# Decoding order in the first block, a smaller sum of squares, and a third decoding ahead of the first transposes

## The chip, the cores and the metric

The program runs on one core of a Trainium2 chip. The metric is the device time of one execution in microseconds (us). The engines named below are TensorE (PE, matrix products), VectorE (DVE), ScalarE (ACT), GpSimd (POOL) and SyncE (SP, whose queue starts the DMA transfers). Each of them works through its own list of instructions in the order written, and semaphores hold an instruction until what it needs is there.

## The reference

Local-plus-global attention is followed by two feed-forward layers. There are 4 batches of 512 local and 32 global tokens, 2176 in all, and 8 heads of 64, so the width is 512.

```python
s_ll = where(|i - j| <= 32, 0.125 * q_l @ k_l.T, -1e9)          # window of 32 on either side
out_l = softmax([0.125 * q_l @ k_g.T, s_ll]) @ [v_g, v_l]
out_g = softmax(0.125 * q_g @ [k_g, k_l].T) @ [v_g, v_l]
x = [out_g, out_l] as (2176, 512)
h = x @ w_in                                  # 512 -> 2048
x = where(h > 0, h, exp(min(h, 0)) - 1) @ w_out          # 2048 -> 512
xn = x / sqrt(mean(x * x) + 1e-6) * rms_g
g = xn @ w_gate;  out = (g * sigmoid(g) * (xn @ w_val)) @ w_o2      # 512 -> 1536 -> 512
```

The weights reach the chip as 64-bit floats, and the kernel decodes them there into 32-bit floats by integer operations.

## The kernel before

**Numbers as two halves.** Every operand of a large product is kept as a high half in the format fp32r and a low half (what the high half leaves over), and a product is three matmuls: high by high, high by low, low by high (`PASSES`). ScalarE makes a high half by a copy, VectorE the low half by a subtraction.

**Decoding a weight piece.** A piece holds 2 x 128 rows by 512 columns. `dec_abs` (line 79, ScalarE) takes the absolute value of the upper word into `dx`; `dec_bits` (lines 86 to 89, VectorE) clamps, shifts, and puts in the sign and the low bits; `w1_hi` (line 92, ScalarE) makes the high half in `wA`, `w1_lo` (line 95, VectorE) the low half. Each waits for the one before. In the text a decoding's six instructions are called abs, clamp, shift, sign, low bits (the four of `dec_bits`), and then high and low. Sixteen pieces (0 to 15) belong to the first layer: in each group of four (`order1`) two pieces of `w_in`, needed by four steps of the block, and two of `w_out`, each needed by two steps.

**Order of the first layer.** The attention of the first block's four units (0 to 3) is computed in a list written out by hand, with pieces 0 to 2 laid between. Then `moe_block` runs for four blocks of 512 tokens with 16 steps each. Step j computes `h` (12 matmuls, line 128), its activation on ScalarE and VectorE (`elu_a`, lines 117 to 119, then `g`, lines 135 and 136), and the second product of the step before (`y`, 12 matmuls, line 142). Beside it, every four steps take one unit of the next block's attention: scores `s` and their row maxima (lines 229 and 230) and exponentials `E` (line 232) at the first step, transposes and their copies `ET` (line 240) at the second, the product with v at the third. In block 0 every step 0 to 12 ends with `w1_decode`, which decodes one more piece (3 to 15) and starts a later transfer.

**What sets the order.** TensorE's list is in program order throughout, and in the first stretch (the list by hand) ScalarE's and VectorE's too. From block 0 on, a scheduler orders the instructions of ScalarE and VectorE by when it reckons them ready; with `tc.keep_in_program_order` an instruction may not move ahead of those written before it on its engine. Blocks 1 and 2 decode the second layer's weights (with that mark already) and store them to memory, from where the second layer fetches them (`w2_fetch`).

**Second layer.** `prep` makes the normalised `xn` in four parts: load, sum of squares over the four column groups (ScalarE squares, GpSimd adds into `acc`), a product with a matrix of ones that sums over partitions (`ms`, line 558), and the scaling.

Of the kernel before, what the change touches and what calls it, by code (L numbers as in the profile page):

```python
# [34 lines left out]
def i32(ap):  # L35
    return ap.bitcast(I32)
# [3 lines left out]
def fused_kernel(ctx: ExitStack, tc: tile.TileContext, kq, vl, gkq, gv, w_in, w_out, w_gate, w_val, w_o2, rms_g, consts, out):  # L40
# [36 lines left out]
    def dec_abs(pool, raw, keep=False):  # L77
        x = pool.tile([P, 1024], F32, tag="dx", name="dx")
        ins = nc.scalar.activation(x, f(words(raw)[:, :, 1]), AF.Abs)  # L79
        if keep:  # L80
            tc.keep_in_program_order(ins)
        return x

    def dec_bits(x, raw):
        word = words(raw)
        nc.vector.tensor_scalar(out=x, in0=x, scalar1=HI_MIN, scalar2=HI_MAX, op0=ALU.max, op1=ALU.min)
        nc.vector.tensor_scalar(out=i32(x), in0=i32(x), scalar1=3, scalar2=0x3FFFFFFF, op0=ALU.logical_shift_left, op1=ALU.bitwise_and)
        nc.vector.scalar_tensor_tensor(out=i32(x), in0=word[:, :, 1], scalar=-0x40000000, in1=i32(x), op0=ALU.bitwise_and, op1=ALU.bitwise_or)  # L88
        nc.vector.scalar_tensor_tensor(out=i32(x), in0=word[:, :, 0], scalar=29, in1=i32(x), op0=ALU.logical_shift_right, op1=ALU.bitwise_or)  # L89

    def split_hi(dst, t):
        nc.scalar.copy(dst[:, :, 0, :], t.rearrange("p (a n) -> p a n", a=2))
# [80 lines left out]
    with ExitStack() as ls:  # L173
# [176 lines left out]
        dxs, dsts = {}, {}  # L350

        def w1_abs(i):
            dxs[i] = dec_abs(dec["t"], raws[i])

        def w1_bits(i):
            dec_bits(dxs[i], raws.pop(i))

        def w1_hi(i):
            kind, a, G = order1[i]
# [9 lines left out]
        def w1_lo(i):  # L369
            split_lo(dsts.pop(i), dxs.pop(i))  # L370
            n_dec[0] = i + 1
# [14 lines left out]
        with tc.manual_schedule(engines={mybir.EngineType.DVE, mybir.EngineType.Activation}):  # L386
            nc.scalar.copy(identr, ident)
            nc.scalar.copy(masks, mk)
            load_kq(1)
            load_v(1)  # L390
            w1_load()
            load_kq(2)
            load_v(2)
            load_kq(3)
            load_v(3)
            w1_load(3)
            w1_abs(0)
            a_S(0, ATT2)
            w1_bits(0)
            a_E(0)  # L400
            a_S(1, HB)
            a_T(0, 0, yps, "y0")
            a_T(0, 1, yps, "y1")
            w1_hi(0)
            a_E(1)
            a_PV(0, Y2)
            w1_lo(0)
            a_N(0)
            w1_abs(1)
            a_S(2, ATT2)  # L410
            a_T(1, 0, yps, "y0")
            a_T(1, 1, yps, "y1")
            a_E(2)
            w1_bits(1)
            a_PV(1, Y2)
            a_N(1)
            a_S(3, HB)
            a_T(2, 0, yps, "y0")
            a_T(2, 1, yps, "y1")
            a_E(3)  # L420
            w1_hi(1)
            a_PV(2, Y2)
            a_N(2)
            a_T(3, 0, yps, "y0")
            a_T(3, 1, yps, "y1")
            w1_lo(1)
            w1_abs(2)
            a_PV(3, Y2)
            a_N(3)
            xT_t = {0: new_xT()}  # L430
            a_X(0, (0, 1), xT_t[0], ATT2[:2] + HB)
            last = a_X(0, (2, 3), xT_t[0], ATT2[:2] + HB)
            w1_bits(2)
            w1_hi(2)
            w1_lo(2)
        w1_load(2)
# [21 lines left out]
        def slot0(j, part, h):  # L458
            g = act1(h, 512, elu_a) if part == 0 else None
            att_slot(0, j, part)  # L460
            if part == 2:
                with tc.issue_after(last[0].ins), tc.issue_after(last[1].ins):
                    w1_decode()
                if j == 12:
                    w2_load()
                    w2_load()
            return g
# [24 lines left out]

    def second_start():
        bpools["bp"] = ctx.enter_context(tc.tile_pool(name="bp", bufs=1))
        bpools["ones"] = bpools["bp"].tile([P, P], F32, name="ones")
        nc.sync.dma_start(out=bpools["ones"], in_=consts[:, 4 * P:5 * P])
        bpools["gg"] = stage.enter_context(tc.tile_pool(name="ggp", bufs=2))
        bpools["st"] = stage.enter_context(tc.tile_pool(name="bst", bufs=4))
        prep(0, 0)
        w2_fetch()  # L500

    wraws, n_fetch = [], [0]

    def w2_fetch():
        while len(wraws) < 4 and n_fetch[0] < 18:
            raw = bpools["st"].tile([P, 1024], F32, tag="wraw", name="wraw")
            i = n_fetch[0]
            nc.sync.dma_start(out=raw.rearrange("p (a n) -> p a n", a=2), in_=wT[2 * i:2 * i + 2].rearrange("a p n -> p a n"))
            wraws.append(raw)
            n_fetch[0] += 1  # L510
# [24 lines left out]
    def prep(k, part):  # L535
# [8 lines left out]
        elif part == 1:  # L544
# [3 lines left out]
            for c in range(1, 4):  # L548
# [3 lines left out]
                    sq = moe.tile([P, 512], F32, tag="e", name="sq", bufs=2)  # L552
                nc.scalar.activation(sq[:, :n], y32[:, c, :n], AF.Square)
                nc.gpsimd.tensor_tensor(out=acc[:, :n], in0=acc[:, :n], in1=sq[:, :n], op=ALU.add)
            acc_t[k] = acc
        elif part == 2:
            ms = hps.tile([P, 512], F32, tag="h", name="ms")
            nc.tensor.matmul(ms[:, :n], bpools["ones"], acc_t[k][:, :n], start=True, stop=True)
            rs = stg.tile([P, 512], F32, tag="stg", name="rs")
            nc.scalar.activation(rs[:, :n], ms[:, :n], AF.Sqrt, bias=eps, scale=1.0 / DM)  # L560
            nc.vector.reciprocal(rs[:, :n], rs[:, :n])
# [349 lines left out]
```

## Time and profile before

| what | us |
|---|---|
| median of 3 runs (lowest, highest) | 949.61 (947.6, 949.84) |
| the profiled execution's own time | 949.2 |
| its span, first to last instruction | 947.3 |
| TensorE busy in the span | 915.8 |
| VectorE busy in the span | 459.7 |
| ScalarE busy in the span | 347.0 |

Durations of single instructions come from the profiled execution, so sums are made against its 949.2 us. A table by stretches gives for each engine the time in which it was busy and, behind x, the instructions begun in it; `PEclk` is the granted TensorE clock as a share of full speed. In a timeline, a number in brackets at a row's end is the time for which the engine was idle ahead of it and what ended that.

### The profile page before, as it was taken

How to read it: one execution, taken by the hardware profiler on the slowest of the kernel's cores; microseconds unless marked ns; L12 is line 12 of the kernel's file. 1: busy time of each engine (PE TensorE's matmuls, PEld its weight loads, DVE VectorE, ACT ScalarE, POOL GpSimd, SP SyncE). 2: the span in 40 equal slices, each digit the busy share in tenths (PEclk: the TensorE clock that was granted, in tenths of full speed). 3: DMA queues.
4: the chain of work that ended last, by engine and by line, in shares of the span. 5: the costliest groups of instructions: out<-in, count | busy, mean ns of one | idle time of the engine just before them, and what ended most of it. 6: DMA issues, size and time to landing. Idle time of an engine off the chain costs nothing.

```text
span 947.3 us, 15710 instructions
## 1 busy us (share of the span) xinstructions
PE 915.8 (97%) x6738; PEld 766.5 (81%) x6738; DVE 459.7 (49%) x791; ACT 347.0 (37%) x627; POOL 17.9 (2%) x19
## 2 busy tenths in 40 slices
PE   6788899999999999999999999999999999999997
PEld 5566688888887788777888888888889999999996
DVE  4799963666578874543786215221412241142111
ACT  4577544434443443332656213122312232232111
POOL 0000000000000000000100100001000100100000
PEclk9999999999999999999999999999999999999999
DMA  9675541544567763351644000100011010000000
GB/s 364 250 297 188 178 163 57 181 170 166 187 223 277 276 232 127 124 184 57 243 137 157 12 1 5 41 33 1 1 34 45 1 34 34 1 1 34 1 1 34
DMA packets 34445, 107.77 MB, mean 114 GB/s; under 512 B 3016, under 2 KB 5704, under 8 KB 31816
## 3 DMA queue, kind: packets, MB, share of 16 engines
q1 hardware_dynamic: 34376, 106.77, 31.5%
q8 instruction: 53, 0.87, 0.4%
q14 instruction: 16, 0.13, 0.0%
HBM read 88.41 MB, written 18.35 MB: 113 GB/s over the span
## 4 chain that ended last, share of the span: by engine, by line
PE 84%; DVE 8%; DMA 3%; issue 2%; ACT 2%; SPq 0%; ACTq 0%
PE y L142 15%; PE pg L633 15%; PE pv L633 15%; PE y L639 15%; PE h L128 14%; DVE dx L88 1%; DVE dx L89 1%; PE o L251 1%; PE yg L597 1%; PE s L221 1%; PE hg L581 1%; PE ptp L238 1%; DMA kq<-in_kq 1%; PE s L216 1%; DVE wA L95 1%
## 5 line engine op out<-in xcount | busy, mean ns | idle before, releaser
L142 PE MATMUL y<-g,wA 128*128 128x512 f32 x768 | 198.8, 402 | 6.1 <-DVE g L136 5.7
L128 PE MATMUL h<-xT,wA 128*128 128x512 f32 x768 | 186.8, 392 | 1.3 <-DVE xT L276 1.3
L142 PEld LDWEIGHTS y<-g,wA 128*128 128x128 f32 x768 | 140.2, 189 | 40.9 <-DVE g L136 8.4
L128 PEld LDWEIGHTS h<-xT,wA 128*128 128x128 f32 x768 | 144.2, 189 | 32.3 <-DVE xT L276 1.5
L806 DVE TENSOR_TENSOR silu<-pv,silu 128x384 f32<-128x384 f32 (+1 forms) x60 | 36.7, 611 | 257.2 <-PE pv L633 249.1
L639 PE MATMUL y<-wB,p 128*128 128x512 f32 x612 | 149.0, 391 | 0.0
L639 PEld LDWEIGHTS y<-wB,p 128*128 128x128 f32 x612 | 114.4, 188 | 22.3
L805 ACT ACTIVATE silu<-pg 128x384 f32<-128x384 f32 (+1 forms) x60 | 32.1, 534 | 158.9 <-PE pg L633 158.7
L633 PE MATMUL pv<-xT,wB 128*128 128x384 f32 (+1 forms) x432 | 88.4, 352 | 0.0
L633 PEld LDWEIGHTS pv<-xT,wB 128*128 128x128 f32 x432 | 77.3, 188 | 5.6
L808 ACT CAST p<-silu 128x384 fp32r<-128x384 f32 (+1 forms) x60 | 33.3, 555 | 127.0 <-DVE silu L806 126.8
L135 ACT CAST g<-e 128x512 fp32r<-128x512 f32 x64 | 39.8, 622 | 75.8 <-DVE e L111 71.0
L633 PE MATMUL pv<-xnB,wB 128*128 128x512 f32 (+1 forms) x288 | 61.5, 362 | 0.0
L109 ACT ACTIVATE e<-h 128x512 f32<-128x512 f32 x48 | 28.9, 601 | 85.3 <-PE h L128 77.9
L633 PE MATMUL pg<-xT,wB 128*128 128x384 f32 (+1 forms) x288 | 60.1, 357 | 0.0
L633 PEld LDWEIGHTS pg<-xT,wB 128*128 128x128 f32 x288 | 52.1, 188 | 5.8 <-issue 0.5
L633 PEld LDWEIGHTS pv<-xnB,wB 128*128 128x128 f32 x288 | 52.2, 188 | 5.6
L809 DVE TENSOR_TENSOR p<-silu,p 128x384 fp32r<-128x384 f32 (+1 forms) x60 | 38.0, 634 | 35.5 <-ACT p L808 35.5
L110 DVE TENSOR_SCALAR e<-e 128x512 f32<-128x512 f32 x52 | 22.2, 428 | 65.2 <-ACT e L109 65.0
L136 DVE TENSOR_TENSOR g<-e,g 128x512 fp32r<-128x512 f32 x64 | 45.1, 705 | 17.6 <-ACT g L135 16.3
L79 ACT ACTIVATE dx<-raw 128x1024 f32<-128x1024 f32 x34 | 39.5, 1162 | 10.9 <-DMA raw<-in_moe_w_out 4.3
L232 ACT ACTIVATE E<-s,mx 128x128 f32<-128x128 f32 x128 | 35.1, 384 | 22.3 <-DVE mx L230 22.3
(179 smaller groups left out, 948.5 us busy)
## 6 DMA issues: line engine op xcount, KB each, us to landing
raw<-in_moe_w_out SPq DMA_DIRECT2D x14, 1024.0 KB, 6.1
wT<-dx SPq DMA_DIRECT2D x18, 512.0 KB, 3.4
wraw<-wT SPq DMA_DIRECT2D x18, 512.0 KB, 4.2
raw<-in_moe_w_in SPq DMA_DIRECT2D x8, 1024.0 KB, 7.2
raw<-in_moe_w_gate SPq DMA_DIRECT2D x6, 1024.0 KB, 6.2
raw<-in_moe_w_val SPq DMA_DIRECT2D x6, 1024.0 KB, 6.8
gvr<-in_gv SPq DMA_DIRECT2D x8, 640.0 KB, 4.6
gkq<-in_gkq SPq DMA_DIRECT2D x4, 1152.0 KB, 5.2
```

What stands on the lines that cost most here:

```text
L79: ins = nc.scalar.activation(x, f(words(raw)[:, :, 1]), AF.Abs)
L128: nc.tensor.matmul(h[:, :n], W1[c, G][:, ws, o:o + P], xT[c][:, xs, :n], start=(k == 0), stop=(k == 11))
L135: nc.scalar.copy(g[:, 0, :n], e[:, :n])
L136: nc.vector.tensor_tensor(out=g[:, 1, :n], in0=e[:, :n], in1=f(g[:, 0, :n]), op=ALU.subtract)
L142: nc.tensor.matmul(ys[dc][:, :n], W2[j][:, ws, dc * P:(dc + 1) * P], g[:, gs, :n], start=(j == 0 and k == 0), stop=(j == 15 and k == 2))
L232: nc.scalar.activation(e[par][:, pr, :], ss[par][:, pr, :], AF.Exp, bias=mx[:, par, pr:pr + 1], scale=SCALE)
L633: nc.tensor.matmul(ps[:, :n], W[c, G3][:, ws, o:o + P], xn[c][:, xs, :n], start=(k == 0), stop=(k == 11))
L639: nc.tensor.matmul(os_[t], p[:, pp, t * P:(t + 1) * P], Wo[j][:, ww, :], start=(j == 0 and k == 0), stop=(j == 11 and k == 2))
L805: nc.scalar.activation(s[:, :n], pg[:, :n], AF.Silu)
L806: nc.vector.tensor_tensor(out=s[:, :n], in0=pv[:, :n], in1=s[:, :n], op=ALU.mult)
L808: nc.scalar.copy(p[:, 0, :n], s[:, :n])
L809: nc.vector.tensor_tensor(out=p[:, 1, :n], in0=s[:, :n], in1=f(p[:, 0, :n]), op=ALU.subtract)
```

## The change

Four things change. First, in block 0 the abs of pieces 3 to 15 carries the mark that keeps it in ScalarE's written order, and `w1_decode` as a whole is held back behind one instruction of the last transposes instead of two. Second, the decoding of piece 2 moves in the list by hand from behind the transposes of x to between the last attention units: its abs ahead of the exponentials of unit 3, its four bit steps apart among the normalisations of units 2 and 3. Third, the sum of squares is split into high and low halves and multiplied by fp32r ones in two matmuls, where one fp32 matmul stood. Fourth, the ones are set by GpSimd instead of being loaded, and the buffers for the fetched weights go from 4 to 3.

```diff
--- before.py
+++ after.py
@@ -81,12 +81,16 @@
             tc.keep_in_program_order(ins)
         return x
 
-    def dec_bits(x, raw):
+    def dec_bits(x, raw, steps=range(4)):
         word = words(raw)
-        nc.vector.tensor_scalar(out=x, in0=x, scalar1=HI_MIN, scalar2=HI_MAX, op0=ALU.max, op1=ALU.min)
-        nc.vector.tensor_scalar(out=i32(x), in0=i32(x), scalar1=3, scalar2=0x3FFFFFFF, op0=ALU.logical_shift_left, op1=ALU.bitwise_and)
-        nc.vector.scalar_tensor_tensor(out=i32(x), in0=word[:, :, 1], scalar=-0x40000000, in1=i32(x), op0=ALU.bitwise_and, op1=ALU.bitwise_or)
-        nc.vector.scalar_tensor_tensor(out=i32(x), in0=word[:, :, 0], scalar=29, in1=i32(x), op0=ALU.logical_shift_right, op1=ALU.bitwise_or)
+        if 0 in steps:
+            nc.vector.tensor_scalar(out=x, in0=x, scalar1=HI_MIN, scalar2=HI_MAX, op0=ALU.max, op1=ALU.min)
+        if 1 in steps:
+            nc.vector.tensor_scalar(out=i32(x), in0=i32(x), scalar1=3, scalar2=0x3FFFFFFF, op0=ALU.logical_shift_left, op1=ALU.bitwise_and)
+        if 2 in steps:
+            nc.vector.scalar_tensor_tensor(out=i32(x), in0=word[:, :, 1], scalar=-0x40000000, in1=i32(x), op0=ALU.bitwise_and, op1=ALU.bitwise_or)
+        if 3 in steps:
+            nc.vector.scalar_tensor_tensor(out=i32(x), in0=word[:, :, 0], scalar=29, in1=i32(x), op0=ALU.logical_shift_right, op1=ALU.bitwise_or)
 
     def split_hi(dst, t):
         nc.scalar.copy(dst[:, :, 0, :], t.rearrange("p (a n) -> p a n", a=2))
@@ -350,10 +354,10 @@
         dxs, dsts = {}, {}
 
         def w1_abs(i):
-            dxs[i] = dec_abs(dec["t"], raws[i])
-
-        def w1_bits(i):
-            dec_bits(dxs[i], raws.pop(i))
+            dxs[i] = dec_abs(dec["t"], raws[i], keep=i > 2)
+
+        def w1_bits(i, steps=range(4)):
+            dec_bits(dxs[i], raws[i] if 3 not in steps else raws.pop(i), steps)
 
         def w1_hi(i):
             kind, a, G = order1[i]
@@ -417,20 +421,22 @@
             a_S(3, HB)
             a_T(2, 0, yps, "y0")
             a_T(2, 1, yps, "y1")
+            w1_abs(2)
             a_E(3)
+            w1_bits(2, (0, 1))
             w1_hi(1)
             a_PV(2, Y2)
             a_N(2)
             a_T(3, 0, yps, "y0")
             a_T(3, 1, yps, "y1")
+            w1_bits(2, (2,))
             w1_lo(1)
-            w1_abs(2)
             a_PV(3, Y2)
             a_N(3)
+            w1_bits(2, (3,))
             xT_t = {0: new_xT()}
             a_X(0, (0, 1), xT_t[0], ATT2[:2] + HB)
             last = a_X(0, (2, 3), xT_t[0], ATT2[:2] + HB)
-            w1_bits(2)
             w1_hi(2)
             w1_lo(2)
         w1_load(2)
@@ -459,7 +465,7 @@
             g = act1(h, 512, elu_a) if part == 0 else None
             att_slot(0, j, part)
             if part == 2:
-                with tc.issue_after(last[0].ins), tc.issue_after(last[1].ins):
+                with tc.issue_after(last[1].ins):
                     w1_decode()
                 if j == 12:
                     w2_load()
@@ -492,17 +498,17 @@
 
     def second_start():
         bpools["bp"] = ctx.enter_context(tc.tile_pool(name="bp", bufs=1))
-        bpools["ones"] = bpools["bp"].tile([P, P], F32, name="ones")
-        nc.sync.dma_start(out=bpools["ones"], in_=consts[:, 4 * P:5 * P])
+        bpools["ones"] = bpools["bp"].tile([P, P], F32R, name="ones")
+        nc.gpsimd.memset(f(bpools["ones"]), 1.0)
         bpools["gg"] = stage.enter_context(tc.tile_pool(name="ggp", bufs=2))
-        bpools["st"] = stage.enter_context(tc.tile_pool(name="bst", bufs=4))
+        bpools["st"] = stage.enter_context(tc.tile_pool(name="bst", bufs=3))
         prep(0, 0)
         w2_fetch()
 
     wraws, n_fetch = [], [0]
 
     def w2_fetch():
-        while len(wraws) < 4 and n_fetch[0] < 18:
+        while len(wraws) < 3 and n_fetch[0] < 18:
             raw = bpools["st"].tile([P, 1024], F32, tag="wraw", name="wraw")
             i = n_fetch[0]
             nc.sync.dma_start(out=raw.rearrange("p (a n) -> p a n", a=2), in_=wT[2 * i:2 * i + 2].rearrange("a p n -> p a n"))
@@ -552,10 +558,15 @@
                     sq = moe.tile([P, 512], F32, tag="e", name="sq", bufs=2)
                 nc.scalar.activation(sq[:, :n], y32[:, c, :n], AF.Square)
                 nc.gpsimd.tensor_tensor(out=acc[:, :n], in0=acc[:, :n], in1=sq[:, :n], op=ALU.add)
-            acc_t[k] = acc
+            a2 = bpools["bp"].tile([P, 2, 512], F32R, tag="a2", name="a2")
+            nc.scalar.copy(a2[:, 0, :n], acc[:, :n])
+            nc.vector.tensor_tensor(out=a2[:, 1, :n], in0=acc[:, :n], in1=f(a2[:, 0, :n]), op=ALU.subtract)
+            acc_t[k] = a2
         elif part == 2:
             ms = hps.tile([P, 512], F32, tag="h", name="ms")
-            nc.tensor.matmul(ms[:, :n], bpools["ones"], acc_t[k][:, :n], start=True, stop=True)
+            acc = acc_t[k]
+            for i in range(2):
+                nc.tensor.matmul(ms[:, :n], bpools["ones"], acc[:, i, :n], start=(i == 0), stop=(i == 1))
             rs = stg.tile([P, 512], F32, tag="stg", name="rs")
             nc.scalar.activation(rs[:, :n], ms[:, :n], AF.Sqrt, bias=eps, scale=1.0 / DM)
             nc.vector.reciprocal(rs[:, :n], rs[:, :n])
```

The names in the next rows are the program's: `e_1061` is the activation of step 5 in block 0, `e_957` that of step 4, `E_1009` and `E_1010` the exponentials of attention unit 5, and `dx_1037`, `dx_1094`, `dx_1180` hold pieces 7, 8 and 9.

ScalarE in steps 4 and 5 of block 0, before:

```order
L79 ACTIVATE dx_1037<-raw_755 128x1024
L117 ACTIVATE e_914<-h_901 128x512
L118 ACTIVATE e_914<-e_914 128x512
L135 CAST g_918<-e_914 128x512
L92 CAST wA_939<-dx_933 128x2x512
L117 ACTIVATE e_957<-h_944 128x512
L118 ACTIVATE e_957<-e_957 128x512
L79 ACTIVATE dx_1094<-raw_812 128x1024
L92 CAST wA_1043<-dx_1037 128x2x512
L135 CAST g_961<-e_957 128x512
L79 ACTIVATE dx_1180<-raw_899 128x1024
L232 ACTIVATE E_1009<-s_964,mx_1008 128x128 x4
```

ScalarE at the same place in the changed kernel:

```order
L139 CAST g_961<-e_957 128x512
L236 ACTIVATE E_1009<-s_964,mx_1008 128x128 x4
L236 ACTIVATE E_1010<-s_965,mx_1008 128x128 x4
L79 ACTIVATE dx_1037<-raw_755 128x1024
L121 ACTIVATE e_1061<-h_1048 128x512
L96 CAST wA_1043<-dx_1037 128x2x512
L122 ACTIVATE e_1061<-e_1061 128x512
L244 COPY ET_1079<-ptp_1074 128x512
L244 COPY ET_1086<-ptp_1081 128x512
L79 ACTIVATE dx_1094<-raw_812 128x1024
L139 CAST g_1065<-e_1061 128x512
L121 ACTIVATE e_1118<-h_1105 128x512
```

The abs of piece 7 (`dx_1037`) stood ahead of step 3's activation and now stands behind the exponentials of step 4. The abs of piece 8 (`dx_1094`) stood in step 4 and now stands in step 5, behind the copies `ET` and ahead of that step's `g_1065`; the abs of piece 9 is no longer in the first six steps.

VectorE from the low half of piece 6 on, before:

```order
L95 TENSOR_TENSOR wA_939<-dx_933,wA_939 128x2x512
L89 SCALAR_TENSOR_TENSOR dx_1037<-raw_755,dx_1037 128x1024
L119 SCALAR_TENSOR_TENSOR e_957<-e_957,h_944 128x512
L86 TENSOR_SCALAR dx_1094<-dx_1094 128x1024
L95 TENSOR_TENSOR wA_1043<-dx_1037,wA_1043 128x2x512
L229 TENSOR_REDUCE mx_1008<-s_964 128x4
L87 TENSOR_SCALAR dx_1094<-dx_1094 128x1024
L229 TENSOR_REDUCE mx_1008<-s_965 128x4
L136 TENSOR_TENSOR g_961<-e_957,g_961 128x512
L230 TENSOR_SCALAR mx_1008<-mx_1008 128x4
L86 TENSOR_SCALAR dx_1180<-dx_1180 128x1024
L88 SCALAR_TENSOR_TENSOR dx_1094<-raw_812,dx_1094 128x1024
```

VectorE at the same place in the changed kernel:

```order
L99 TENSOR_TENSOR wA_939<-dx_933,wA_939 128x2x512
L140 TENSOR_TENSOR g_961<-e_957,g_961 128x512
L233 TENSOR_REDUCE mx_1008<-s_964 128x4
L233 TENSOR_REDUCE mx_1008<-s_965 128x4
L234 TENSOR_SCALAR mx_1008<-mx_1008 128x4 x2
L87 TENSOR_SCALAR dx_1037<-dx_1037 128x1024
L89 TENSOR_SCALAR dx_1037<-dx_1037 128x1024
L91 SCALAR_TENSOR_TENSOR dx_1037<-raw_755,dx_1037 128x1024
L93 SCALAR_TENSOR_TENSOR dx_1037<-raw_755,dx_1037 128x1024
L99 TENSOR_TENSOR wA_1043<-dx_1037,wA_1043 128x2x512
L123 SCALAR_TENSOR_TENSOR e_1061<-e_1061,h_1048 128x512
L87 TENSOR_SCALAR dx_1094<-dx_1094 128x1024
```

Before, steps of two or three pieces alternate and lie between the row maxima (`mx_1008`). Now the maxima come in one run, then the whole of piece 7 in a row, its bit steps and its low half next to each other, and only then the activation of step 5.

ScalarE ahead of the first block, before:

```order
L232 ACTIVATE E_497<-s_438,mx_496 128x128 x4
L232 ACTIVATE E_498<-s_439,mx_496 128x128 x4
L92 CAST wA_511<-dx_318 128x2x512
L240 COPY ET_559<-ptp_554 128x512
L240 COPY ET_566<-ptp_561 128x512
L79 ACTIVATE dx_569<-raw_129 128x1024
L275 CAST xT0_612<-xtp_616 128x512
L275 CAST xT1_613<-xtp_623 128x512
L275 CAST xT2_614<-xtp_630 128x512
L275 CAST xT3_615<-xtp_637 128x512
L79 ACTIVATE dx_746<-raw_131 128x1024
```

ScalarE at that place in the changed kernel:

```order
L79 ACTIVATE dx_496<-raw_129 128x1024
L236 ACTIVATE E_499<-s_438,mx_498 128x128 x4
L236 ACTIVATE E_500<-s_439,mx_498 128x128 x4
L96 CAST wA_515<-dx_318 128x2x512
L244 COPY ET_563<-ptp_558 128x512
L244 COPY ET_570<-ptp_565 128x512
L279 CAST xT0_616<-xtp_620 128x512
L279 CAST xT1_617<-xtp_627 128x512
L279 CAST xT2_618<-xtp_634 128x512
L279 CAST xT3_619<-xtp_641 128x512
L96 CAST wA_648<-dx_496 128x2x512
```

The abs of piece 2 (`dx_569`, now `dx_496`) has moved from behind the copies of unit 3 to ahead of its exponentials, and the abs of piece 3 no longer follows the four casts of xT.

## Rows read from the trace of the kernel before

**Rows 1.** The page: busy time by engine, and the group of all abs instructions.
```profile
PE 915.8 (97%) x6738; PEld 766.5 (81%) x6738; DVE 459.7 (49%) x791; ACT 347.0 (37%) x627; POOL 17.9 (2%) x19
...
L79 ACT ACTIVATE dx<-raw 128x1024 f32<-128x1024 f32 x34 | 39.5, 1162 | 10.9 <-DMA raw<-in_moe_w_out 4.3
```

**Rows 2.** Table by stretches: length, PE, PEld, DVE, ACT, POOL busy, PEclk, DMA.
```profile
43.20:118.40 75.20, 66.28 (x616) 51.91 (x614) 74.96 (x105) 49.22 (x80) 0.00 (x0) 0.98 0.58 209
71.84:102.95 31.11, 27.61 (x251) 21.73 (x250) 31.07 (x45) 21.64 (x33) 0.00 (x0) 1.00 0.55 193
102.95:134.02 31.07, 28.56 (x251) 22.82 (x250) 26.79 (x38) 17.82 (x31) 0.00 (x0) 0.95 0.54 194
134.02:162.33 28.31, 28.31 (x267) 23.43 (x266) 10.64 (x23) 12.51 (x27) 0.00 (x0) 1.00 0.19 65
189.06:215.58 26.52, 26.52 (x252) 21.77 (x250) 16.80 (x30) 9.91 (x21) 0.00 (x0) 1.00 0.54 192
```

**Rows 3.** TensorE's longest wait from 42 to 135 us: total, times, longest.
```profile
PE y L142 <- DVE g L136: 5.3, 4, 2.5
```

**Rows 4.** Chain of waits around two products with ones: start, duration, what.
```profile
481.29 2.72 PE y L142 x12
484.87 2.97 PE h L128 x12
...
675.27 2.72 PE y L639 x12
678.64 2.77 PE pg L633 x12
```

**Rows 5.** Timeline ahead of block 0: start, duration, engine, line, tiles.
```profile
32.72 0.59 ACT L240 COPY ET<-ptp 128x512 f32<-128x512 f32 x1 [2.41 <-PE ptp L238]
33.22 2.17 ACT L232 ACTIVATE E<-s,mx 128x128 f32<-128x128 f32 x8
...
37.11 1.29 ACT L79 ACTIVATE dx<-raw 128x1024 f32<-128x1024 f32 x1
...
42.63 3.01 PE L128 MATMUL h<-xT,wA 128*128 128x512 f32 x12 [1.29 <-DVE xT L276]
```

**Rows 6.** VectorE's groups by line, 43.2 to 118.4 us: busy, mean ns.
```profile
L88 DVE SCALAR_TENSOR_TENSOR dx<-raw,dx 128x1024 int32<-128x1024 int32 x13 | 15.9, 1226 | 0.1
L89 DVE SCALAR_TENSOR_TENSOR dx<-raw,dx 128x1024 int32<-128x1024 int32 x12 | 14.6, 1217 | 0.0
L95 DVE TENSOR_TENSOR wA<-dx,wA 128x1024 fp32r<-128x1024 f32 x12 | 14.6, 1216 | 0.0
L87 DVE TENSOR_SCALAR dx<-dx 128x1024 int32<-128x1024 int32 x13 | 8.9, 688 | 0.1
L86 DVE TENSOR_SCALAR dx<-dx 128x1024 f32<-128x1024 f32 x13 | 8.8, 685 | 0.1
```

**Rows 7.** Timeline: one high half, then one undisturbed step of block 0.
```profile
49.02 1.05 ACT L92 CAST wA<-dx 128x1024 fp32r<-128x1024 f32 x1 [2.07 <-DVE dx L89]
...
136.94 0.60 ACT L117 ACTIVATE e<-h 128x512 f32<-128x512 f32 x1 [2.81 <-PE h L128]
137.57 0.63 ACT L118 ACTIVATE e<-e 128x512 f32<-128x512 f32 x1
138.24 0.69 DVE L119 SCALAR_TENSOR_TENSOR e<-e,h 128x512 f32<-128x512 f32 x1 [3.37 <-ACT e L118]
138.96 0.62 ACT L135 CAST g<-e 128x512 fp32r<-128x512 f32 x1 [0.75 <-DVE e L119]
140.22 1.28 DVE L229 TENSOR_REDUCE mx<-s 128x4 f32<-128x512 f32 x2
141.67 2.17 ACT L232 ACTIVATE E<-s,mx 128x128 f32<-128x128 f32 x8 [2.10 <-DVE mx L230]
```

**Rows 8.** Table by stretches of 1 us, columns as in rows 2.
```profile
55.00:56.00 1.00, 1.00 (x5) 0.69 (x4) 1.00 (x2) 1.00 (x5) 0.00 (x0) 0.50 1.08 444
...
121.00:122.00 1.00, 1.00 (x4) 0.74 (x3) 0.97 (x2) 1.00 (x3) 0.00 (x0) 0.50 0.47 147
```

## The prediction

> **What bounds the kernel now.** I read the page first: TensorE is busy for 915.8 of 947.3 us [rows 1], so time is to be had where it idles, or by taking work from it. The table by stretches says where it idles. Four steps late in the first layer take 26.52 us and TensorE works through all of it: that is what four steps with one attention unit cost when nothing is late. In block 0 the same piece of work took 31.11 us in steps 4 to 7 and 31.07 in steps 8 to 11, and from step 12 to the end of the block 28.31 us without idling [rows 2]. VectorE was busy for 74.96 of the 75.20 us from 43.20 to 118.40. So block 0 is held by VectorE's queue, and the longest single wait of TensorE there is for the low half of g, up to 2.5 us [rows 3]. That queue holds the decoding of the weights: a piece costs it 0.69 + 0.69 + 1.23 + 1.22 + 1.22 = 5.0 us [rows 6].
>
> **The change part by part.**
>
> *Products with ones.* From the start of a y product to the start of the next one with an ordinary one between (12 matmuls, 2.72 us, 0.227 each) there are 3.58 us in two cases and 3.37 in three: the fp32 product costs 0.86 us at 512 columns and 0.65 at 384 [rows 4]. Two fp32r matmuls cost 2 x 0.227 = 0.45, or 0.34 at 384 by the share of columns. Gain: 2 x 0.41 + 3 x 0.31 = 1.7 us, all on TensorE's path, since it idles nowhere there. The Trainium skill, "FP8 and Floating Point Precision", TensorE Precision Notes, says that a true fp32 product makes four passes through the array; by that a product would cost 4 x 0.227 = 0.91 us and the gain would be 1.9 instead of 1.7; the rows, at 3.8 passes, decide. The halves added for it are a ScalarE copy as for g (0.62, rows 7) and a VectorE subtraction (half of the 1.22 of a low half of double size, rows 6, so 0.6), five times. They lie between two parts of `prep` that are two steps of TensorE's products apart; without that cover each would cost 1.2 us. Ones by a memset and three buffers in place of four: a fetch starts one piece later. No row prices that; the nearest is a high half's 1.05 us [rows 7], by which a late piece would push what is queued behind it. I take 0, bounds -0.3 and +1.0.
>
> *Piece 2 ahead of x.* On ScalarE its abs (1.16 us, rows 1) now stands between the copies of unit 2's transposes and the eight exponentials of unit 3, which started at once when it was not there [rows 5]. Behind them queue unit 3's transposes, its product with v, x and xT: all of it 1.1 us later. On VectorE the last bit step (1.22) lies between x and the low halves of xT and adds 0.2. So block 0 starts 1.3 us later than 42.63. Bounds: 0, if the exponentials had slack that the trace doesn't show, and +5, if the raw weights landed only just before 37.11, where their abs ran in the kernel before (37.11 - 33.22 = 3.9 more).
>
> *Steps 0 to 3.* VectorE no longer has eight bit steps of pieces 2 and 3 ahead of the first g, and the 2.5 us wait goes. Late next: the attention product of step 2, by 0.4, and the g of step 2, by 1.1 us, behind the bit steps of piece 4. From the first h to the h of step 4: 26.52 less one y product (2.72) that step 0 doesn't have, plus 1.5, is 25.3 us; the trace has 71.84 - 42.63 = 29.2. Gain 3.9.
>
> *From step 4 on: ScalarE's order.* The trace's timeline follows the printed order row by row on both engines, so I laid the rows' durations end to end along it, each instruction starting when its predecessor and what it needs are done. Two things happen. The abs now follows the exponentials, so VectorE sits idle after the row maxima for 2.2 + 1.16 us, and where a piece's low half follows its bit steps directly it waits again for the high half (1.05, rows 7): idle time put into the queue that was 99% busy. And a decoding of the second w_in piece of a group (5, 9, 13) has only one step of lead, so TensorE stands in the middle of h in steps 4, 8 and 12 until its high and low half are there. The chain from that wait in step 8 to the one in step 12, with small latencies in the terms:
> rest of h 0.9; activation 0.60 + 0.63, high and low half of piece 10 and g low, 4.3 in all; row maxima 1.4; exponentials 2.2; abs 1.1; the four bit steps 3.9; high half 1.1; activation 0.5 and two copies 1.0; abs 1.1, clamp 0.7, g low 0.6; the rest of y 2.5 and h 2.7; wait for an abs 0.4, activation 1.3, then its VectorE part behind shift and sign 1.9 + 0.7, g high 0.6; abs 1.1, high half of piece 13 1.0; behind a shift 0.4, low half 1.2 [rows 6, 7]. Sum 32.6 us, against 31.07 traced and 26.52 undisturbed. From step 4 to 8 it is 1.7 more, since the wait in step 4 is 4.8 us (high half 3.6, low half 1.2) instead of 3.1, piece 5's abs standing behind the late g of step 2 and its high half behind the g of step 3 and one more abs: 34.3 against 31.11. Behind step 12, 28.31 plus that step's wait of 3.1.
>
> *Sum.* +1.3 - 3.9 + 3.2 + 1.5 + 3.1 = +5.2 us in block 0. The same laying of the kernel before ends its block at 160.0 us where the trace has 162.33; 1.0 of that is the clock (below), the other 1.3 are latencies too small to list, and I add them. The granted clock stood at 0.50, that is at 1.2 instead of 2.4 GHz, in the microseconds after two stretches of waiting, near 55 and 121 us [rows 8]. A mean clock of 0.95 over the 31.07 us of steps 8 to 11 [rows 2] is 1.6 us lost to such a stretch. Behind the wait in step 4, longer than the longest now [rows 3], I expect it again; part of it falls where TensorE would wait anyway, and I take 1.0. Together +7.5, less 1.7: 949.2 + 5.8 = 955.0 us. The profiled execution's 949.2 is 0.4 below the median of 949.61, which I leave out.
>
> **The rivals.**
>
> *Half clock behind all three waits.* The Trainium skill, "TensorE: Matmul & The Clock Gate", Part 1, has it that the half-rate clock is the default and activity releases it, so that idling brings it back; what it would make of the time is this rival. For it: the trace has it twice already [rows 8], and the waits in steps 8 and 12 are 3.1 us with two matmuls between their parts. Two more stretches, each costing its whole 1.6 because behind them nothing else is late, make 3.2: 958.2. Against it: the waits there are shorter than that of step 4, and TensorE's mean clock from 43.20 to 118.40 was 0.98 though it idled for 8.9 us [rows 2].
>
> *VectorE's sum decides.* Its 3.8 us for piece 2 leave block 0, and if the rest stays as dense as now, TensorE's 8.9 us of idling shrink by that: 949.2 - 3.8 + 1.3 - 1.7 = 945.0. For it: 74.96 of 75.20 us. It decides if VectorE idles in the block for less than those 3.8 us. Against it: in the printed order the maxima, the exponentials, the abs and the bit steps form one chain with nothing of VectorE's between, four times over.
>
> *A trade.* The new waits only replace those for g, as they do up to step 4, where the changed kernel is ahead by 3.9 - 1.3 = 2.6 us. It decides when the waits in steps 4, 8 and 12 are 2 us each instead of 4.8, 3.1 and 3.1: of the 7.5 us there remain 2.5, and the products take 1.7 back: 950.0. For it: a tenth or two too much in each of the 23 terms would do. Against it: the h of step 4 has its wait for both halves written in the middle of its products, and their predecessors are not ready.
>
> **How the numbers follow.** Forecast 0.50 (952.5 to 957.5), half clock three times 0.19, trade 0.18, VectorE's sum 0.13. A measurement of this kernel tells 0.3%, 2.9 us, from no change: slower is above 952.5. So slower 0.69, same 0.18, faster 0.13. The range from 948.5 to 959.5 leaves out the faster rival and the ends of the others; the likeliest case alone spans 952.5 to 957.5.
>
> **What would show it.** In the profile after: h of step 4 should be cut in two by a wait for the high half (ScalarE) of 3 to 4 us and one of about 1 for the low half, and likewise shorter in steps 8 and 12; VectorE should be idle for some 3 us after each run of row maxima in block 0 and busy clearly below 99% there; block 0 should begin near 44.0 us and end near 168 to 172 instead of 162.33; the products with ones should take half as long. If VectorE stays fully busy to 118 us, or TensorE passes step 4 without a wait, the forecast is wrong; if block 0 begins after 45 us, the transfer of piece 2 was late.

## The result and the profile after

The changed kernel took 958.64 us in the median of three runs (957.34 to 960.8) against 949.61 us. The ratio is 1.0105, 95% interval 1.0077 to 1.0134, so it is slower by about 1%. Its profiled execution took 957.34 us, with a span of 955.4.

The first table by stretches has the approach to block 0 and then its four groups of steps (steps 0 to 3, 4 to 7, 8 to 11, 12 to the end), columns as in [rows 2]. The groups end at the first `h` of steps 4, 8, 12 and of block 1.

```profile
38.00:45.05 7.05, 5.83 (x80) 4.86 (x80) 6.48 (x12) 2.98 (x7) 0.00 (x0) 0.52 0.25 70
45.05:70.63 25.58, 24.69 (x238) 19.58 (x239) 18.63 (x30) 15.72 (x28) 0.00 (x0) 1.00 0.56 204
70.63:106.01 35.38, 30.44 (x252) 23.30 (x250) 28.61 (x41) 18.15 (x30) 0.00 (x0) 0.90 0.51 183
106.01:139.48 33.47, 29.16 (x251) 22.78 (x250) 27.64 (x40) 18.28 (x31) 0.00 (x0) 0.95 0.34 117
139.48:171.89 32.41, 30.46 (x267) 24.31 (x266) 22.41 (x35) 17.77 (x32) 0.00 (x0) 0.95 0.45 153
```

Block 0 begins at 45.05 us instead of 42.63 [rows 5] and ends at 171.89 instead of 162.33 [rows 2]: 9.56 us lost. Behind it the kernel takes 783.51 us against 784.97, 1.46 less. Steps 0 to 3 gained 3.63 us against this row of the kernel before:

```profile
42.63:71.84 29.21, 26.29 (x238) 20.50 (x239) 29.11 (x43) 18.86 (x31) 0.00 (x0) 0.94 0.64 242
```

Against [rows 2], the later groups lost 4.27, 2.40 and 4.10. VectorE, full before in the first two groups of steps, is now idle for 7 us in each; in the third it is idle for 6 us, where it was for 4.

The table of waits in block 0 of the changed kernel names what TensorE and VectorE waited for (total, times, longest). TensorE:

```profile
PE h L132 <- ACT wA L96: 6.0, 3, 3.3
PE h L132 <- DVE wA L99: 2.3, 3, 0.9
PE y L146 <- DVE g L140: 2.1, 4, 0.8
PE y L146 <- ACT g L139: 1.2, 2, 1.0
```

VectorE:

```profile
DVE dx L87 <- ACT dx L79: 15.0, 7, 3.2
DVE wA L99 <- ACT wA L96: 3.7, 7, 1.1
```

Waits for g fell from 5.3 us [rows 3] to 3.3, and `h` now waits 8.3 us for weights, which it did not in the kernel before; and VectorE now waits 15.0 us for an abs, where the kernel before had this:

```profile
DVE dx L86 <- ACT dx L79: 0.4, 1, 0.4
```

The timeline at the first row maxima shows how:

```profile
51.38 1.28 DVE L233 TENSOR_REDUCE mx<-s 128x4 f32<-128x512 f32 x2
52.58 0.28 DVE L234 TENSOR_SCALAR mx<-mx 128x4 f32<-128x4 f32 x2
52.83 2.18 ACT L236 ACTIVATE E<-s,mx 128x128 f32<-128x128 f32 x8 [2.09 <-DVE mx L234]
54.85 1.20 ACT L79 ACTIVATE dx<-raw 128x1024 f32<-128x1024 f32 x1
56.08 0.70 DVE L87 TENSOR_SCALAR dx<-dx 128x1024 f32<-128x1024 f32 x1 [3.21 <-ACT dx L79]
```

Maxima, eight exponentials, abs, clamp stand in one chain, and VectorE has nothing else in it. TensorE's timeline in the `h` of steps 4, 8 and 12, and, between the last two, ahead of the `y` that stands in step 10 and takes the g of step 9:

```profile
75.49 1.22 PE L132 MATMUL h<-xT,wA 128*128 128x512 f32 x2 [3.34 <-ACT wA L96]
77.15 2.08 PE L132 MATMUL h<-xT,wA 128*128 128x512 f32 x4 [0.44 <-DVE wA L99]
...
109.21 0.73 PE L132 MATMUL h<-xT,wA 128*128 128x512 f32 x2 [1.68 <-ACT wA L96]
110.87 1.19 PE L132 MATMUL h<-xT,wA 128*128 128x512 f32 x4 [0.92 <-DVE wA L99]
...
128.97 0.51 PE L146 MATMUL y<-g,wA 128*128 128x512 f32 x1 [0.98 <-ACT g L139]
129.79 4.38 PE L146 MATMUL y<-g,wA 128*128 128x512 f32 x11 [0.32 <-DVE g L140]
...
142.02 0.73 PE L132 MATMUL h<-xT,wA 128*128 128x512 f32 x2 [1.02 <-ACT wA L96]
143.68 2.07 PE L132 MATMUL h<-xT,wA 128*128 128x512 f32 x4 [0.92 <-DVE wA L99]
```

Each of the three `h` is cut in two as forecast. The last four matmuls of each take 1.19 us in step 8 and 2.07 to 2.08 in steps 4 and 12. The table by 1 us gives the clock at five places, the last during step 8's wait:

```profile
42.00:43.00 1.00, 1.00 (x6) 1.00 (x5) 0.94 (x2) 0.73 (x2) 0.00 (x0) 0.50 0.00 0
77.00:78.00 1.00, 0.85 (x2) 0.76 (x3) 1.00 (x2) 0.00 (x0) 0.00 (x0) 0.50 0.00 0
131.00:132.00 1.00, 1.00 (x4) 0.77 (x3) 1.00 (x3) 0.00 (x0) 0.00 (x0) 0.50 1.02 433
145.00:146.00 1.00, 1.00 (x4) 0.69 (x3) 1.00 (x1) 0.21 (x1) 0.00 (x0) 0.50 0.00 0
108.00:109.00 1.00, 0.00 (x0) 0.00 (x0) 0.96 (x3) 1.00 (x2) 0.00 (x0) 1.00 0.00 0
```

The clock fell behind the waits of steps 4 and 12, behind the wait for the g of step 9 (0.98 + 0.32 us), and ahead of block 0; not behind step 8's wait of 2.60 us (1.68 + 0.92). In steps 0 to 3 it stayed at 1.00, where the kernel before had a mean of 0.94.

The chain of waits around the product with ones, which answers to [rows 4]:

```profile
491.46 2.72 PE y L146 x12
494.18 0.45 PE ms L569 x2
494.64 2.72 PE h L132 x12
```

From the start of `y` to the start of the `h` behind it there are 3.18 us instead of 3.58: 0.40 less, where 0.41 was worked out.

### The profile page after: what moved, and what is told of

It reads as the page before. It is cut to its first block, busy times and chain, and to the rows that moved or that the text cites. A ratio compares the mean times of both kernels' runs of the same rounds, so it can differ in the third digit from the quotient of the medians.

```text
span 955.4 us, 15712 instructions
## 1 busy us (share of the span) xinstructions
PE 920.2 (96%) x6738; PEld 770.5 (81%) x6738; DVE 466.5 (49%) x796; ACT 348.7 (36%) x632; POOL 18.6 (2%) x20
## 4 chain that ended last, share of the span: by engine, by line
PE 82%; DVE 9%; ACT 4%; DMA 3%; issue 2%; SPq 0%; ACTq 0%
PE pg L644 15%; PE pv L644 15%; PE y L650 15%; PE y L146 14%; PE h L132 14%; DVE dx L93 1%; DVE dx L91 1%; PE yg L608 1%; PE s L225 1%; PE hg L592 1%; PE o L255 1%; DMA kq<-in_kq 1%; PE s L220 1%; ACT dx L79 1%; PE ptp L242 1%
## 5 line engine op out<-in xcount | busy, mean ns | idle before, releaser
L132 PE MATMUL h<-xT,wA 128*128 128x512 f32 x768 | 189.7, 395 | 8.9 <-ACT wA L96 6.0
L87 DVE TENSOR_SCALAR dx<-dx 128x1024 f32<-128x1024 f32 x34 | 23.5, 692 | 43.4 <-ACT dx L79 43.2
```

The costliest lines, as they stand in the source:

```text
L132: nc.tensor.matmul(h[:, :n], W1[c, G][:, ws, o:o + P], xT[c][:, xs, :n], start=(k == 0), stop=(k == 11))
```

## The experiments

Ratios are against runs of the kernel before on the same chip, whose median was 949.0 to 949.6 us each time. The stages, in us, are of each kernel's one profiled execution: first `h`, the four groups of steps, the end of block 0. That execution can lie off the median: e9's took 952.2 us, e11's 942.2.

| kernel | median us | ratio (95%) | first h | 0–3 | 4–7 | 8–11 | 12–end | end |
|---|---|---|---|---|---|---|---|---|
| before | 949.61 | 1 | 42.63 | 29.21 | 31.11 | 31.07 | 28.31 | 162.33 |
| changed | 958.64 | 1.0105 (1.0077–1.0134) | 45.05 | 25.58 | 35.38 | 33.47 | 32.41 | 171.89 |
| e1 | 957.63 | 1.0086 (1.0070–1.0103) | 43.51 | 31.00 | 26.53 | 33.22 | 37.28 | 171.54 |
| e2 | 950.98 | 1.0014 (1.0003–1.0024) | 45.35 | 33.91 | 28.61 | 28.90 | 28.33 | 165.10 |
| e3 | 948.14 | 0.9989 (0.9981–0.9998) | 43.71 | 29.18 | 31.80 | 31.06 | 28.32 | 164.07 |
| e4 | 949.99 | 1.0014 (1.0004–1.0025) | 44.87 | 32.51 | 28.62 | 28.90 | 28.33 | 163.23 |
| e5 | 953.92 | 1.0049 (1.0034–1.0064) | 44.01 | 29.85 | 28.92 | 33.97 | 28.33 | 165.08 |
| e6 | 945.55 | 0.9957 (0.9943–0.9971) | 45.38 | 30.14 | 27.11 | 26.76 | 28.48 | 157.87 |
| e7 | 954.54 | 1.0054 (1.0037–1.0070) | 46.08 | 26.18 | 38.66 | 29.84 | 28.33 | 169.09 |
| e8 | 955.17 | 1.0061 (1.0041–1.0080) | 44.15 | 26.21 | 36.38 | 27.05 | 35.99 | 169.78 |
| e9 | 949.78 | 1.0004 (0.9993–1.0015) | 44.80 | 27.80 | 34.98 | 30.27 | 28.33 | 166.18 |
| e10 | 947.94 | 0.9981 (0.9970–0.9992) | 43.99 | 25.96 | 38.06 | 26.54 | 28.32 | 162.87 |
| e11 | 944.22 | 0.9943 (0.9929–0.9956) | 41.87 | 26.11 | 31.10 | 26.54 | 29.36 | 154.98 |
| e12 | 943.40 | 0.9932 (0.9918–0.9947) | 42.96 | 26.07 | 32.46 | 26.80 | 29.35 | 157.64 |
| e13 | 955.72 | 1.0079 (1.0064–1.0093) | 44.83 | 25.70 | 35.35 | 33.43 | 30.93 | 170.24 |
| e14 | 954.48 | 1.0064 (1.0051–1.0077) | 43.30 | 31.00 | 26.51 | 33.22 | 33.21 | 167.24 |

### One part at a time

**e1**, the mark alone:

```diff
-            dxs[i] = dec_abs(dec["t"], raws[i])
+            dxs[i] = dec_abs(dec["t"], raws[i], keep=i > 2)
...
-                with tc.issue_after(last[0].ins), tc.issue_after(last[1].ins):
+                with tc.issue_after(last[1].ins):
```

> The kernel before with the mark on the abs of pieces 3 to 15 (and the one hold-back instead of two), nothing else of the change. Theory A, the mark: it puts the abs behind the exponentials and gives the second w_in piece of each group one step of lead, so TensorE waits in h of steps 4, 8 and 12; these groups cost +4.3, +2.4 and +4.1 us as in the changed kernel, and of the 3.6 us won in steps 0 to 3 about half stays, since piece 2 is still decoded behind x: 949.6 + 10.8 - 1.8 = 958.6 us (956.5 to 960.5), with first h near 42.6 us. Theory B, the late start: block 0's trouble comes from piece 2's abs ahead of unit 3's exponentials, which starts the block 2.4 us late at half clock; then the mark alone changes nothing: 949.6 us (948 to 951).

957.63: theory A's time. Its stages were wrong: the first four steps were not shorter, and then steps 4 to 7 ran undisturbed while step 12 was hit harder. The mark costs the time; why it strikes in other steps than in the changed kernel no run settles.

**e2**, piece 2 alone:

```diff
+            w1_abs(2)
             a_E(3)
+            w1_bits(2, (0, 1))
...
+            w1_bits(2, (2,))
             w1_lo(1)
-            w1_abs(2)
...
+            w1_bits(2, (3,))
...
-            w1_bits(2)
```

> The kernel before with piece 2's decoding moved in the list by hand, nothing else. Theory A: the start of block 0 is late by 2.4 us, VectorE has 3.8 us less ahead of the first g, and from step 4 on the order is free as before: 949.6 + 2.4 - 1.8 = 950.2 us (948.5 to 951.5), first h near 45.0 us, no wait for a high half over 1 us in h of steps 4, 8 and 12. Theory B: the waits in h come with the late start: 949.6 + 9.6 = 959 us (957 to 960.5).

950.98, and no wait in `h` for weights: theory B falls. The first four steps became longer (33.91): without the mark ScalarE does four abs, and VectorE most of their bit steps, ahead of unit 4's exponentials, which begin at 60.73 us instead of 52.83 in the changed kernel, and TensorE waits for exponentials:

```profile
PE ptp L242 <- ACT E L236: 5.8, 4, 3.4
```

**e3**, the products, with the ones set by GpSimd and three buffers for the fetched weights (of its edit, the matmuls):

```diff
-            nc.tensor.matmul(ms[:, :n], bpools["ones"], acc_t[k][:, :n], start=True, stop=True)
+            acc = acc_t[k]
+            for i in range(2):
+                nc.tensor.matmul(ms[:, :n], bpools["ones"], acc[:, i, :n], start=(i == 0), stop=(i == 1))
```

> The kernel before with the sum of squares in two fp32r products, ones set by GpSimd, and three fetch buffers, nothing else; block 0 as before. Both theories: the products take 1.7 us from TensorE, all on its path, and of the traced difference of the rest of the kernel, -1.46, this is all: 949.6 - 1.5 = 948.1 us (947.3 to 949.2). If three buffers make a fetch late: 949 to 950.5.

948.14, a gain of 0.1% (0.02 to 0.19%): about 1.0 us. Behind block 0 its profile takes 947.2 - 164.07 = 783.13 us, 1.84 less than before.

**e4**, all but the mark:

```diff
-            dxs[i] = dec_abs(dec["t"], raws[i], keep=i > 2)
+            dxs[i] = dec_abs(dec["t"], raws[i])
```

> The changed kernel without the mark (piece 2 moved, products in two halves, one hold-back kept). Theory A: the waits in h of steps 4, 8 and 12 go, the late start stays: 949.6 + 2.4 - 1.8 - 1.5 = 948.7 us (946.5 to 950). Theory B: the waits stay, since the late start stays: 957.5 us (956 to 959.5).

949.99, at the upper end of theory A. Without the mark 8.7 us of the loss are gone, though the single hold-back stays, so it is the mark that costs; VectorE's wait for an abs falls from 15.0 to 1.4 us.

### Deadline or idle VectorE

**e5**, one step more of lead, mark kept:

```diff
                     w1_decode()
+                    if j == 0:
+                        w1_decode()
```

> The changed kernel with two decodings instead of one at the end of step 0, so that every later piece is decoded one step earlier; the mark stays. Theory D (deadline): what costs is that the second w_in piece of a group has one step of lead; with two, the waits of 6.0 + 2.3 us in h of steps 4, 8 and 12 go, and the half clock behind two of them, about 3 us, goes with them: 958.6 - 11.3 = 947.3 us (946 to 951). Theory I (idle VectorE): what costs is that VectorE stands 15.0 us waiting for an abs behind exponentials; that stays, the waits move from h to y, and the time stays at 956 us or more.

953.92, between the theories. The waits in `h` for weights are gone, and waits for g have come instead, as theory I had it:

```profile
PE y L146 <- DVE g L140: 6.0, 4, 2.3
PE y L146 <- ACT g L139: 3.0, 2, 1.8
```

VectorE's wait for an abs was halved (7.5 us), and so was the loss.

**e6**, the same mark, but each abs written at the start of its step:

```diff
-                w1_abs(i)
                 w1_bits(i)
...
+            if part == 0 and n_dec[0] < 16:
+                w1_abs(n_dec[0])
             g = act1(h, 512, elu_a) if part == 0 else None
```

> The changed kernel with each abs of pieces 3 to 15 written at the start of its step, ahead of the activation and the exponentials, instead of at its end; the mark stays, and the bit steps stay where they were. Theory I: VectorE's 15.0 us of waiting for an abs fall to under 3, block 0 is as dense as before: 947 to 950 us. Theory D: only the part of the lateness that is the abs goes, 1.2 to 3.2 us of each chain, against waits in h of 4.6, 2.6 and 1.9 us; the first remains by a third: 951 to 954 us.

945.55, better than theory I said, and faster than both kernels. Its stretches from step 4 on:

```profile
75.52:102.63 27.11, 26.87 (x252) 21.70 (x251) 25.82 (x38) 18.15 (x30) 0.00 (x0) 1.00 0.52 183
102.63:129.39 26.76, 26.76 (x252) 21.77 (x250) 25.50 (x39) 18.28 (x30) 0.00 (x0) 1.00 0.56 186
129.39:157.87 28.48, 28.48 (x268) 23.42 (x267) 18.11 (x31) 15.82 (x30) 0.00 (x0) 1.00 0.42 138
```

These are almost the undisturbed 26.52 and 28.31 of [rows 2], with the piece order, the mark and the step of every piece's bit steps as in the changed kernel. The place of the abs behind the exponentials is thus what costs; with the abs ahead of them the short lead costs nothing here, and with it behind them one step more of lead (e5) saves half.

**e7**, the mark on pieces 3 and 4 alone (`keep=i in (3, 4)`), and **e8**, on all but 5, 9 and 13 (`keep=i > 2 and i not in (5, 9, 13)`):

> The changed kernel with the mark on pieces 3 and 4 alone. The first four steps should go as in the changed kernel (25.6 us from first h to the h of step 4, against 32.5 without any mark), since only there the mark keeps the abs of later pieces from standing ahead of unit 4's exponentials. From step 4 on, theory D: the pieces are free to go ahead again, the waits in h go, and these steps take 28.6 + 28.9 + 28.3 us as without the mark: block 1 begins near 156.5, and the time is 950.0 - 6.7 = 943.3 us (942 to 946). Rival: VectorE, which did 31.7 us of work in the first four steps without the mark and 18.6 with it, has to make up 13 us by step 12, the gain is given back, and the time is 948 to 950 us.

> The changed kernel with the mark on all of pieces 3 to 15 but 5, 9 and 13, the second w_in piece of each group. Theory D: these three may go ahead again, the waits in h go and with them the half clock: 947 us (945 to 951). Theory I: the other ten abs still stand behind the exponentials and VectorE still waits for them: 955 us or more.

954.54 and 955.17. In e7 the first four steps were short as expected and the next four took 38.66 us, so both expectations were too low: more was given back than the rival had it. In e8 VectorE still waits 14.2 us for an abs, and the time is theory I's: 3.5 of the 9.0 us of loss are gone. To free the piece that is late gives back only a part when VectorE stood idle before it.

### Towards a faster kernel

**e9**, e6 with the abs of piece 3 left at the end of step 0 (`part == 0 and j > 0`); **e10**, e9 with piece 2's abs one place earlier:

```diff
             a_T(2, 0, yps, "y0")
+            w1_abs(2)
             a_T(2, 1, yps, "y1")
-            w1_abs(2)
```

> As the run with each abs at the start of its step, except that the abs of piece 3 stays at the end of step 0, behind the exponentials of unit 4. In that run the first four steps took 30.1 us instead of 25.6, with TensorE waiting 2.5 us for those exponentials behind the bit steps of piece 3. Theory: the first four steps take 26 to 27.5 us, steps 4 to 7 up to 1.5 us more than the 27.1 there, since VectorE has about 4 us of work to make up and 1.3 us of idling left to do it in: 945.6 - 2.5 = 943.1 us (941.5 to 945). Rival: all of it is made up with TensorE waiting: 945 to 947 us.

> The kernel just above, and in the list by hand the abs of piece 2 stands one place earlier, between the two copies of unit 2's transposes, where ScalarE idles for 2.1 us. If the start of block 0 is late because this abs pushes unit 3's exponentials, block 0 starts 1.2 us earlier, at about 43.8 instead of 45.0, and the time is 1.2 us shorter than that kernel's. If the raw weights of piece 2 land only by 32 to 33 us, the second copy is pushed instead and nothing is won or up to 1 us is lost.

e9 is no gain (949.78): both expectations fell. The single abs of piece 3 behind exponentials, 3.2 us of idle VectorE, is enough for a wait of 2.7 + 0.5 us in the `h` of step 4. In e10 block 0 starts 0.8 us earlier than in e9 (1.2 expected) and the time is 1.8 shorter; its groups differ by more than that in both directions, so the start is not separated from the rest here.

**e11**, the kernel before with e6's early, marked abs and nothing else of the change; **e12**, e11 with the products of e3:

> The kernel before with the mark on the abs of pieces 3 to 15, each written at the start of its step; piece 2 and the products as before. Theory: a mark whose place is ahead of the exponentials does no harm; against the 945.6 us of the run with the rest of the change, 1.5 us of the products come back, and VectorE has the 3.8 us of piece 2 to do in block 0, which starts 1.7 us earlier for it: 945.6 + 1.5 + 3.8 - 1.7 = 949.2 us (947 to 950.5), no wait in h for a high half. Rival: the mark costs whatever its place, and only piece 2's move pays for it: 953 us or more.

> The kernel of the last run (the mark, each abs at the start of its step, piece 2 where it was) with the products of the change. If the two parts add, as theory has it, since the products lie in the second layer and the abs in block 0: 944.2 - 1.0 to 1.7 = 942.5 to 943.2 us, a ratio near 0.993. If the earlier end of block 0 brings other waits behind it: 944 us or more.

e11: 944.22. Its mark does no harm, as the theory had it, but the size was 5 us off: I had charged it for piece 2's bit steps on VectorE, and its first four steps take 26.11 us all the same. e12, 943.40 us, 0.2 above its forecast, is the best of all, 0.68% faster than the kernel before (0.53 to 0.82%). No run has the early abs without the mark, so what part of the gain is the mark's and what part the place's is not shown. Why e11 does not need piece 2 moved, while e6 with it takes 30.14 us in the same steps, is not settled: the scheduler's order differs in more than one place.

### What the half clock costs

**e13** fills the changed kernel's wait in step 12 by issuing the first six products of `h` twice; **e14** does it in e1, three times:

```diff
+        for r in range(again):
+            for c in range(2):
+                for ws, xs in PASSES:
+                    nc.tensor.matmul(h[:, :n], W1[c, G][:, ws, o:o + P], xT[c][:, xs, :n], start=(c == 0 and ws == PASSES[0][0] and xs == PASSES[0][1]), stop=(c == 1 and (ws, xs) == PASSES[2]))
```

> The changed kernel with the first six products of h in step 12 of block 0 issued twice (1.4 us at full clock, the second time with a fresh start, so the sum is the same), which fills most of the 1.94 us that TensorE waits there. Theory C (the clock costs): the half clock at 143 to 148 us does not come, and the steps from 12 to the end of the block take 32.4 - 1.6 = 30.8 us (30.5 to 31.4); 957.2 us. Rival N (the slow stretch lies beside other lateness): they take 32.4 us as before, or up to 0.4 more, whatever the clock; 958.6 to 959 us.

> The kernel before with the mark alone, and the first six products of h in step 12 issued three times (2.7 us more at full clock) in a wait of 3.4 + 0.9 us. Without them the clock stood at 0.50 from 139 to 150 us, which is 5.3 us of full-clock time lost, and the steps from 12 to the end took 37.3 us. Theory C: the half clock does not come or is short, and they take 32.5 to 34 us; 957.6 - 4 = 953.5 us. Rival N: 37 us or more; 957 to 959 us.

Theory C holds in both. In e13 the last group falls from 32.41 to 30.93 us, the span from 955.4 to 954.0. Its row, and behind it the microsecond in which the clock was 0.50 before the wait was filled:

```profile
139.31:170.24 30.93, 30.04 (x273) 24.45 (x272) 22.35 (x35) 17.64 (x32) 0.00 (x0) 1.00 0.45 161
145.00:146.00 1.00, 1.00 (x65) 0.78 (x64) 0.89 (x1) 0.97 (x3) 0.00 (x0) 1.00 0.00 0
```

In e14 it falls from 37.28 to 33.21. The row of that stretch for e1, and behind it for e14 (columns as above):

```profile
134.26:171.54 37.28, 32.98 (x267) 26.32 (x266) 24.82 (x38) 17.81 (x32) 0.00 (x0) 0.86 0.41 146
```

```profile
134.03:167.24 33.21, 31.67 (x279) 25.52 (x278) 24.53 (x38) 17.91 (x32) 0.00 (x0) 1.00 0.44 160
```

TensorE does 12 matmuls more and is 4.07 us sooner done. Without the repeated products (0.227 us each, [rows 4]) its busy time fell by 1.8 us in e13 and 4.0 in e14, and the groups became 1.5 and 4.1 us shorter: the slow stretch behind a wait costs nearly its whole time here. The Trainium skill, "TensorE: Matmul & The Clock Gate", Part 1, says that the throttled rate is the default and activity releases it; these two traces agree, with a mean clock of 1.00 in both groups where it was 0.95 and 0.86. The rows of step 8 above show a wait of 2.60 us that left the clock at full speed.

## Why the prediction was right in direction and short in size

**What held.** The change made the kernel slower, by the waits worked out: the abs behind the exponentials leaves VectorE idle, the second `w_in` piece comes late, and TensorE stands in the `h` of steps 4, 8 and 12. e1 and e4 show that the mark does it, e6 that it is the place of the abs. The gain in steps 0 to 3 came (3.63, forecast 3.9), and a product with ones is shorter by 0.40 us (forecast 0.41); behind block 0 1.46 of the 1.7 us arrived.

**The step that failed.** It is the term for the clock: 1.0 us, for one slow stretch behind step 4, nothing ahead of block 0 and nothing behind step 12. The runs showed slow products of 2.8 us more in steps 4 to 7, 2.2 more from step 12 on, and 0.6 ahead of block 0. The waits in `h` were put too long by 2.7 us, and that hid a part of it. In the profiled executions the loss is 957.34 - 949.2 = 8.14 us against 5.8. By terms:

- *Start of block 0*: forecast +1.3, measured +2.42, net the largest miss, 1.1 of 2.3 us. I took one abs and 0.2 us of VectorE's as the whole price and one trace's 42.63 as the base. Over the kernels here the first `h` comes at 41.87 to 43.71 us without piece 2's move (six traces, mean 43.0) and at 44.01 to 46.08 with it (nine traces, mean 44.9; e10, with its abs earlier, is not among them), so the start spreads by some 2 us, which one trace can't show. 0.6 us of the miss is the clock, below.
- *The clock*: forecast 1.0 us for a single slow stretch. In the three later groups TensorE's busy time grew by (30.44 + 29.16 + 30.46) - (27.61 + 28.56 + 28.31) = 5.6 us, that is 2.8, 0.6 and 2.2, at mean clocks of 0.90, 0.95 and 0.95 where they had been 1.00, 0.95 and 1.00. e13 and e14 show that such time is lost nearly in full. Against it, the slow stretch that the kernel before had near 55 us [rows 8] is gone: TensorE's busy time in steps 0 to 3 fell by 26.29 - 24.69 = 1.6 us, a part of the gain there.
- *The waits in `h`*: forecast 4.8, 3.1 and 3.1 us; measured 3.78, 2.60 and 1.94, so 2.7 less. TensorE's idle time grew by 11.2 - 6.0 = 5.2 us in the three groups. The two errors nearly cancel: the groups lost 10.8 us where 10.1 were forecast, with the 2.3 us for latencies and clock. That these totals lie so close is luck.
- The rest: 0.3 us in steps 0 to 3, 0.2 behind block 0. Beyond the profiles, the changed kernel's median is 1.3 us above its profiled execution.

**The clock ahead of block 0.** The list by hand is the same in the changed kernel and in e5, where the clock was 1.00 from 38 us to the first `h`:

```profile
34.22 2.17 ACT L236 ACTIVATE E<-s,mx 128x128 f32<-128x128 f32 x8
44.01 3.03 PE L132 MATMUL h<-xT,wA 128*128 128x512 f32 x12 [1.29 <-DVE xT L280]
38.00:44.01 6.01, 3.13 (x81) 2.56 (x75) 5.87 (x13) 2.85 (x6) 0.00 (x0) 1.00 0.20 46
```

From the exponentials of unit 3 to the first `h` e5 takes 9.79 us; e8, with the same list and the clock at 1.00, 9.85. The changed kernel, at 0.52, takes 45.05 - 34.63 = 10.42 us, and e13, at 0.53, 10.45. So the low clock costs 0.6 us there, which no term of the forecast had.

**The rivals.** *Half clock three times* gave 958.2, nearest to the 958.64 (957.34 in the profiled execution). Three slow stretches in block 0 did come, but one of them behind the wait for the g of step 9 and not behind step 8, and with shorter waits than it assumed; that such a stretch costs nearly its whole time, e13 and e14 bear out. *VectorE's sum* fell: VectorE idles 15.0 us for an abs, far over the 3.8 us from which it would not decide. *A trade* fell: it asked for waits of 2 us each, and step 12's 1.94 was the only one, and behind it slow products cost 2.2 us more.

**The test named in the prediction.** Step 4's wait for the high half was 3.34 us (3 to 4 forecast), that for the low half 0.44 (about 1); VectorE was idle for 3.2 us after the first maxima, and waited seven times for an abs in the block; block 0 ended at 171.89 us, within 168 to 172. Block 0 began after 45 us, which I had put down to a late transfer: no row shows ScalarE waiting for the raw weights. In the changed kernel's timeline the abs follows the copy ahead of it at once, and the exponentials follow the abs:

```profile
32.99 0.59 ACT L244 COPY ET<-ptp 128x512 f32<-128x512 f32 x1 [2.14 <-PE ptp L242]
33.48 1.24 ACT L79 ACTIVATE dx<-raw 128x1024 f32<-128x1024 f32 x1
34.63 2.16 ACT L236 ACTIVATE E<-s,mx 128x128 f32<-128x128 f32 x8
```

That reading of a late start was wrong.

## What to carry to other kernels

Keeping an instruction in written order is only as good as its written place: the same mark cost 8.5 us with the abs behind the exponentials (e1) and came with a gain of 4.9 us where the abs stood ahead of the activation (e11). Read from the trace which engine idles for want of that instruction, and move it there before adding lead or freeing single pieces. The Trainium skill, "Perfetto Trace Analysis", Optimization Strategies, advises to work on the engines that TensorE is waiting for; the traces of e5 and e6 agree, and add that one follows the wait a step further back, from TensorE's weights to VectorE's 15.0 us for an abs, which are gone in e6 together with the loss. And where the clock falls behind a wait of TensorE's, the slow products are to be priced with the wait.

## What was not expected of the hardware

In the three later groups the slower products cost as much as the waits: 5.6 us of slower work beside 5.2 us of idling. In these traces the length of a wait did not decide whether the clock fell: behind 1.94 us in step 12 it did, behind 2.60 us in step 8 it did not. Ahead of block 0, where TensorE's busy time was 5.83 us at a mean clock of 0.52 against 3.13 in e5, the low clock cost only 0.6 us: at full clock TensorE stood idle for 2.88 of the 6.01 us there.
